# Turning one batch row's tokens in a single iteration, and re-ordering loads, weight splits and constants in a fused linear-attention and mixture-of-experts kernel

## The chip, the cores and the metric

The kernel runs on one core of a Trainium2 chip. The metric is the device time of one execution in microseconds (us). The kernel before took 807.06 us (median of 3 runs, 805.79 to 808.11).

A core has TensorE (PE in the profile, with its weight loads as PEld), VectorE (DVE), ScalarE (ACT), GpSimd (POOL) and SyncE (SP), which here only issues DMAs. Each engine works through its own instructions in their order and waits at one until what it needs is there; the engines are tied by semaphores only.

## The reference

Three layers follow each other, all in float32:

```
# 1. gated linear attention; B, H, S, D = 4, 8, 768, 48
for t in range(S):
    state = alpha[:, :, t, :, None] * state + einsum('bhd,bhe->bhde', k[:, :, t], v[:, :, t])
    y[:, :, t] = einsum('bhd,bhde->bhe', q[:, :, t], state)
x = y.transpose(0, 2, 1, 3).reshape(3072, 384)
# 2. top-1 mixture of 8 experts, 384 -> 1024 -> 384
e = argmax(x @ w_gate, axis=1);  gate = softmax(x @ w_gate)[e]
x = gate * (relu(x @ w1[e]) @ w2[e])
# 3. dense layer, 384 -> 2048 -> 384
h = x @ w_in;  out = (h * sigmoid(h)) @ w_out
```

## The kernel before, in words

**Attention.** The 32 heads are taken in 16 pairs `p` (4 pairs make one batch row `b`), the 768 steps of a head in 6 chunks of 128. For a pair, DVE runs a scan of alpha forward (`Pf`, step P_SCAN) and one backward (`Rv`, R_SCAN); q is multiplied by the first (`qs`, Q_SCALE, on POOL, for pair 0 on DVE) and k by the second (`ks`, K_SCALE, DVE). TensorE then makes the scores inside a chunk (`Ap`; DVE masks them to `Am`), the state updates (`U`; DVE scans them to `So`, ACT copies them to `Sb`), and the output `Yp` from both. The loop `for p in range(NP + 1)` (NP = 16) is a pipeline written out by hand: iteration p prepares pair p+2, loads pair p+3, makes scores and updates of pair p and the outputs of pair p-1. Nothing reorders it: each engine's order is the order in which the code is written. So "iteration 14" below is the piece of code with p = 14, and iteration 16 only finishes pair 15.

**Routing beside it.** Once the four pairs of a batch row are done, the row's 768 tokens are routed beside the next iterations. `beside_pairs(b)` makes a table from (iteration, place) to steps; `aside(p, place)` runs them. The places in an iteration stand in the order A, F1, F2, F3 (between TensorE's groups), C1 and C2 (around R_SCAN). The steps are: `logits`, `choose` (the largest logit, DVE), `weigh` (`w_exp` on ACT, then `w_gate`, which gives `gt`, on DVE), `ranks`, `slots`, `digits`, `hots`, `invert` and `add` (they build the table `tab` of the tokens of each expert), and six times `rows(b, c)`: TensorE turns a chunk of 128 tokens (`Xt`), ACT scales it by the gate into `xr` (four buffers), SP stores it to `x_d` in DRAM. Batch rows 0 and 1 have five iterations for this; batch row 2 (the `else` branch) has three, 13 to 15. At its end `gather_a` (POOL) fetches up to 192 tokens of the first expert from the stored rows of batch rows 0 to 2 into `xg`; it needs `tab` and all of those stores. Batch row 3 is routed after the loop.

**First expert and after.** In iteration 16 `x_rows` turns the gathered tokens (`xt`, `both`), `logits` makes the logits of batch row 3, and `F1(0, 0, CA)` starts the first expert (line 1095). Its weight tiles come from `w_load(t)` (SP, 384 KB into one of 4 `raw` buffers) and `w_split(t)`, which makes a high part `wh` (ACT) and a low part `wl` (DVE; tile 0 on POOL). Tiles 0 to 3 are loaded in iteration 6; `w_load(t+4)` follows `w_split(t)`, since it takes its buffer. While the first expert runs on 192 tokens, batch row 3 is routed, stored and gathered; then 8 experts and the dense layer follow, all on TensorE.

**Start.** `load(p)` issues alpha, k and q of a pair on SP, `load_v(p)` its v; three pairs are loaded before the loop, pair after pair. POOL sets tiles to zero and, in `constants()` (called in iteration 0), makes the small tables of the routing.

Of the kernel before, what the change touches and what calls it, by code (L numbers as in the profile page):

```python
# [9 lines left out]
F32 = mybir.dt.float32  # L10
# [11 lines left out]
B, H, S, D = 4, 8, 768, 48  # L22
NP = B * H // 2
PA = 112
CH = 128
NC = S // CH
SP = NC * (CH + 1)
# [202 lines left out]
def gla_moe_kernel(  # L230
# [12 lines left out]
    nc = tc.nc  # L243
# [84 lines left out]
    def w_split(t, eng=nc.vector):  # L328
        hi, lo = wslot[slot1(t)]
        nc.scalar.copy(hi, raw[t])  # L330
        eng.tensor_tensor(lo, raw.pop(t), hi.bitcast(F32), op=ALU.subtract)  # L331
# [51 lines left out]
    with actx:  # L383
        ac = actx.enter_context(tc.tile_pool(name="ac", bufs=1, reuse_waits="tile"))
        io = actx.enter_context(tc.tile_pool(name="io", bufs=4, reuse_waits="tile"))
        wk = actx.enter_context(tc.tile_pool(name="wk", bufs=2, reuse_waits="tile"))
        am = actx.enter_context(tc.tile_pool(name="am", bufs=5, reuse_waits="tile"))
        st = {}

        def load(p):  # L390
            if p >= NP:
                return
            a_ = io.tile([PA, SP + 1], F32, tag="a", name="a_", bufs=3)
            nc.sync.dma_start(a_, alpha[p])
            k_ = io.tile([PA, S], F32, tag="k", name="k_", bufs=3)
            nc.sync.dma_start(k_, k[p])
            q_ = io.tile([PA, S], F32, tag="q", name="q_", bufs=3)
            nc.sync.dma_start(q_, q[p])
            st[p] = dict(a=a_, k=k_, q=q_)

        def load_first():

            t = [io.tile([PA, n], F32, tag=x, name=x + "_", bufs=3) for x, n in (("a", SP + 1), ("q", S), ("k", S))]
            for c0, c1 in ((0, SP // 2), (SP // 2, SP + 1)):
                nc.sync.dma_start(t[0][:, c0:c1], alpha[0][:, c0:c1])
            nc.sync.dma_start(t[1], q[0])
            nc.sync.dma_start(t[2], k[0])
            st[0] = dict(a=t[0], q=t[1], k=t[2])

        def load_v(p):  # L410
            if p >= NP:
                return
            st[p]["v"] = v_ = io.tile([128, 2 * NC * D], F32, tag="v", name="v_")
            nc.sync.dma_start(v_, v[p])

        for p in range(3):
            load(p) if p else load_first()
            load_v(p)
        Z1 = ac.tile([PA, SP], F32, name="Z1")
        nc.vector.memset(Z1, TINY)  # L420
        nc.vector.memset(Z1[:, 0 : SP : CH + 1], 1.0)
# [5 lines left out]
        nc.gpsimd.affine_select(  # L427
            out=mask, in_=mask, pattern=[[1, 128]], compare_op=ALU.is_ge, fill=0.0, base=0, channel_multiplier=-1
        )
        for t in [D1[0], W[0], Sb[0], D1[1], W[1]]:  # L430
            nc.gpsimd.memset(t, 0.0)
        wgs = xp.tile([PA, 4, 32], F32, name="wgs", bufs=1)
        nc.sync.dma_start(wgs, wg)
# [2 lines left out]
        iota_i, prow_i = ints[:, 0, :].bitcast(I32), ints[:, 1, 0:NTILE].bitcast(I32)  # L436

        def constants():
            for t in [Sb[1], W[2], W[3]]:
                nc.gpsimd.memset(t, 0.0)  # L440
            nc.gpsimd.memset(bm[:, 0:1], -AHI)
            nc.gpsimd.memset(bm[:, 1:2], ALO)
            nc.gpsimd.iota(iota_i, pattern=[[1, 128]], base=0, channel_multiplier=0)
            nc.gpsimd.iota(prow_i, pattern=[[128, NTILE]], base=0, channel_multiplier=1)
            nc.gpsimd.memset(ones, 1.0)
            nc.gpsimd.memset(onesf, 1.0)
            nc.gpsimd.memset(tri, -1.0)
            nc.gpsimd.affine_select(
                out=tri, in_=tri, pattern=[[-1, 128]], compare_op=ALU.is_ge, fill=0.0, base=0, channel_multiplier=1
            )  # L450
            nc.gpsimd.memset(rmask, 1.0)
            nc.gpsimd.memset(ones8, 1.0)
            nc.gpsimd.memset(rmask[:, :, 0:1], 0.0)
            nc.gpsimd.memset(carry, 0.0)
            nc.gpsimd.tensor_copy(iota_f, iota_i)
            nc.gpsimd.tensor_copy(tokid, prow_i)
            nc.gpsimd.tensor_scalar(w8, iota_f[:, 0:E], -1.0, float(E), op0=ALU.mult, op1=ALU.add)
            nc.gpsimd.tensor_scalar(e512, iota_f[:, 0:E], float(TM), None, op0=ALU.mult)
            nc.gpsimd.tensor_scalar(base, iota_f[:, 0:E], float(NF), None, op0=ALU.mult)
            nc.gpsimd.tensor_copy(keys, w8)  # L460
            nc.gpsimd.memset(keys[:, 0:1], 2.0**17)
            for e in range(E):
                nc.gpsimd.memset(caps[:, e : e + 1], float(CAPS[e]))
# [392 lines left out]
        def f(p, i):  # L856
            if p < NP:
                if p not in prs:
                    prs[p] = prep(p)
                prs[p][i]()  # L860
# [5 lines left out]
        def beside_pairs(b):  # L866
            s_, tb = route(b)
            digits, hots, invert, add = tb
            row = [lambda c=c: rows(b, c) for c in range(NC)]
            p = 4 * b + 5  # L870
            at = {
                (p, "A"): [lambda: logits(b), s_["l_copy"]],
                (p, "F2"): [s_["l_turn"]],
                (p, "F3"): [s_["l_rows"]],
                (p, "C1"): s_["choose"],
            }
            if b < B - 2:
                at |= {
                    (p + 1, "F2"): [s_["ranks"]],
                    (p + 1, "F3"): [s_["w_exp"]],  # L880
                    (p + 1, "C1"): [s_["w_gate"]] + s_["slots"],
                    (p + 1, "C2"): [digits],
                    (p + 2, "F2"): [row[0]],
                    (p + 2, "F3"): [row[1]],
                    (p + 2, "C2"): [hots],
                    (p + 3, "F1"): [row[2]],
                    (p + 3, "F2"): [row[3]],
                    (p + 3, "F3"): [row[4], invert],
                    (p + 3, "C1"): [add],
                    (p + 4, "F1"): [row[5]],  # L890
                }
            else:
                at |= {
                    (p, "C2"): s_["weigh"],
                    (p + 1, "A"): [row[0]],
                    (p + 1, "F1"): [row[1]],
                    (p + 1, "F2"): [row[2]],
                    (p + 1, "F3"): [s_["ranks"]],
                    (p + 1, "C1"): s_["slots"],
                    (p + 1, "C2"): [digits, hots],  # L900
                    (p + 2, "A"): [row[3]],
                    (p + 2, "F1"): [row[4]],
                    (p + 2, "F2"): [row[5], invert, add],
                    (p + 2, "F3"): [gather_a],
                }
            return at

# [9 lines left out]
        for p in range(NP + 1):  # L917
            on, oy = p < NP, p >= 1
            load(p + 3)
            if on:  # L920
                for c in range(0, 3):
                    scores(p, c)
            if p == 0:
                constants()
                f(1, R_SCAN)
            f(p + 1, K_SCALE)

            aside(p, "A")
            if p == NP - 1:
                w_split(0, nc.gpsimd)  # L930
                w_load(4)
            if on:
                ks_transpose(p, 0, 3)
            f(p + 2, P_SCAN)
            aside(p, "F1")
            if oy:
                from_states(p - 1, 0)
            aside(p, "F2")
            if on:
                ks_transpose(p, 3, 5)  # L940
            if oy:
                from_states(p - 1, 1)
            aside(p, "F3")
            if p == 0:
                warm(8)
            f(p + 2, Q_SCALE)
            f(p + 2, DECAY)

            if on:
                for c in range(3, 6):  # L950
                    scores(p, c)
                updates(p, 0, 5)
            if oy:
                within(p - 1, 0)
                within(p - 1, 1)
            if on:
                states(p)
            else:
                y_copy(p - 1, 0)
            if oy:  # L960
                y_copy(p - 1, 1)
            if p == 0:
                warm(6)
            aside(p, "C1")
            f(p + 2, R_SCAN)
            aside(p, "C2")
            for t in {NP - 1: (1, 2), NP: (3,)}.get(p, ()):
                w_split(t)
                w_load(t + 4)
            if not on:  # L970
                x_rows(XG[0], XS[0], 0, 0, 128, bank(2, [128, KD, 128], "xt"))
                x_rows(XG[1], XS[0], 1, 0, CA - 128, bank(0, [128, KD, 128], "xt"))
                logits(B - 1)
                last, last_tb = route(B - 1)
                last["l_copy"]()
            load_v(p + 3)
            if p >= 4 and p % 4 == 0 and p < NP:
                for at, todo in beside_pairs(p // 4 - 1).items():
                    plan_r[at] = plan_r.get(at, []) + todo
            if p == 6:  # L980
                for t in range(4):
                    w_load(t)
# [4 lines left out]
    with mctx:  # L987
# [151 lines left out]
        digits, hots, invert, add = last_tb  # L1139
# [290 lines left out]
```

## Time and profile before

| | |
|---|---|
| median of 3 runs | 807.06 us |
| the profiled execution, time | 807.9 us |
| its span, first to last instruction | 806.2 us |
| busy: PE, DVE, ACT, POOL | 771.3, 491.9, 359.4, 143.6 us |
| mean granted TensorE clock | 0.98 |
| HBM read, written | 69.80, 9.44 MB |

A row of the timeline gives start, length, engine, line, operation, output<-input, shape and count; what stands in brackets is how long the engine had been idle before it and what ended that. Start times count from the start of the span. The granted clock of a stretch is 1.00 at 2.4 GHz and 0.50 at 1.2 GHz.

### The profile page before, as it was taken

Reading aid. Unit: us, or ns where it says so; the run is one execution under the profiler, and the core shown is the slowest. Engines: PE = TensorE matmul, PEld = TensorE weight load, DVE = VectorE, ACT = ScalarE, POOL = GpSimd, SP = SyncE. Lnnn points to the kernel's source line nnn. Section 1 sums busy time; section 2 is a strip of 40 time slices with the busy share of each in tenths; the row PEclk is TensorE's granted clock in tenths of the full one; section 3 lists DMA queues with packets and bytes.
Section 4 is the critical chain, followed back from the end, with each engine's and each line's share of the span. In section 5 each row is a group of like instructions: output and inputs, shape, how many; then the busy total and the mean of one; then the engine's idle time right before and its main releaser. Section 6 shows DMA issues by size and latency. Waiting matters only on the chain. (4 is left out here: it accounts for less than half of the span.)

```text
span 806.2 us, 13071 instructions
## 1 busy us (share of the span) xinstructions
PE 771.3 (96%) x5037; PEld 701.1 (87%) x5037; DVE 491.9 (61%) x836; ACT 359.4 (45%) x683; POOL 143.6 (18%) x178
## 2 busy tenths in 40 slices
PE   7898898689999999999999999999999999999995
PEld 5778777589899999999999999989889998899995
DVE  8999997456878877787778533433343333343332
ACT  1455555334444455555544333544444454333322
POOL 4323331131322312311221120020020002002002
PEclk7899999899999999999999999999999999999998
DMA  9768752343546555655321020031012101001001
GB/s 225 185 196 266 228 164 80 113 159 93 168 142 185 162 171 177 188 174 161 114 79 28 28 74 18 1 91 35 1 48 62 35 1 40 2 1 39 1 1 43
DMA packets 40486, 80.17 MB, mean 99 GB/s; under 512 B 4200, under 2 KB 18423, under 8 KB 40416
## 3 DMA queue, kind: packets, MB, share of 16 engines
q1 hardware_dynamic: 36992, 69.33, 29.2%
q0 software_dynamic: 3424, 9.93, 3.7%
q8 instruction: 41, 0.67, 0.4%
q14 instruction: 29, 0.24, 0.1%
HBM read 69.80 MB, written 9.44 MB: 98 GB/s over the span
## 5 line engine op out<-in xcount | busy, mean ns | idle before, releaser
L1095 PE MATMUL hp<-xh,wh 128*128 128x512 f32 (+9 forms) x504 | 184.8, 369 | 0.0
L1095 PE MATMUL hp<-xh,wl 128*128 128x512 f32 (+9 forms) x504 | 183.7, 368 | 0.9 <-DVE wl L331 0.9
L1269 DVE TENSOR_TENSOR sg<-hp,sg 128x512 f32<-128x512 f32 (+1 forms) x97 | 66.5, 686 | 159.5 <-ACT sg L1268 159.4
L1095 PE MATMUL hp<-xl,wh 128*128 128x512 f32 (+9 forms) x504 | 131.1, 368 | 0.0
L1268 ACT ACTIVATE sg<-hp 128x512 f32<-128x512 f32 (+1 forms) x97 | 57.6, 594 | 156.5 <-PE hp L1095 155.7
L1095 PEld LDWEIGHTS hp<-xh,wh 128*128 128x128 f32 x504 | 94.8, 188 | 10.7 <-issue 0.8
L1095 PEld LDWEIGHTS hp<-xl,wh 128*128 128x128 f32 x504 | 91.7, 188 | 13.9
L1095 PEld LDWEIGHTS hp<-xh,wl 128*128 128x128 f32 x504 | 94.8, 188 | 10.2 <-DVE wl L331 1.1
L1278 DVE TENSOR_TENSOR hl<-sg,hh 128x512 fp32r<-128x512 f32 x95 | 65.8, 692 | 61.9 <-PE ob L1290 41.2
L1277 ACT CAST hh<-sg 128x512 fp32r<-128x512 f32 x95 | 58.9, 620 | 71.1 <-DVE sg L1269 71.1
L1104 ACT ACTIVATE hh<-hp 128x192 fp32r<-128x192 f32 (+8 forms) x72 | 34.5, 479 | 115.2 <-PE hp L1095 115.2
L1309 POOL DMA_INDIRECT out_dram<-o,sidx x24 | 24.2, 1009 | 323.2 <-ACT o L1306 318.9
L1022 POOL TENSOR_TENSOR wl<-dx,wh 128x384 fp32r<-128x384 f32 x32 | 38.4, 1199 | 195.6 <-ACT wh L1019 195.6
L331 DVE TENSOR_TENSOR wl<-raw,wh 128x768 fp32r<-128x768 f32 x63 | 61.1, 972 | 9.1 <-ACT wh L330 8.2
L1106 DVE SCALAR_TENSOR_TENSOR hl<-hp,hh 128x192 fp32r<-128x192 f32 (+8 forms) x72 | 38.9, 540 | 43.5 <-ACT hh L1104 43.2
L1290 PE MATMUL both<-wh,hh 128*128 128x384 f32 x190 | 64.4, 339 | 0.0
L1290 PE MATMUL both<-wh,hl 128*128 128x384 f32 x190 | 64.2, 338 | 0.0
L1290 PE MATMUL both<-wl,hh 128*128 128x384 f32 x190 | 63.9, 337 | 0.0
L1290 PE MATMUL ob<-wl,hh 128*128 128x384 f32 x190 | 63.5, 334 | 0.0
L1290 PE MATMUL ob<-wh,hh 128*128 128x384 f32 x190 | 63.5, 334 | 0.0
L1290 PE MATMUL ob<-wh,hl 128*128 128x384 f32 x190 | 63.5, 334 | 0.0
L330 ACT CAST wh<-raw 128x768 fp32r<-128x768 f32 x64 | 52.9, 828 | 0.1
(394 smaller groups left out, 1483.5 us busy)
## 6 DMA issues: line engine op xcount, KB each, us to landing
raw<-in_wt_dram SPq DMA_DIRECT2D x64, 384.0 KB, 3.4
raw<-in_w_dram SPq DMA_DIRECT2D x32, 384.0 KB, 3.1
raw<-in_alpha_dram SPq DMA_DIRECT2D x16, 336.0 KB, 3.4
x_d<-xr SPq DMA_DIRECT2D x24, 192.0 KB, 3.5
xg<-x_d,gidx POOLq DMA_INDIRECT x29, 3.4
out_dram<-o,sidx POOLq DMA_INDIRECT x24, 2.7
a__140<-in_alpha_dram SPq DMA_DIRECT2D x1, 339.1 KB, 7.4
a__148<-in_alpha_dram SPq DMA_DIRECT2D x1, 339.1 KB, 10.4
```

The lines of the kernel that those rows point to most:

```text
L330: nc.scalar.copy(hi, raw[t])
L331: eng.tensor_tensor(lo, raw.pop(t), hi.bitcast(F32), op=ALU.subtract)
L1022: nc.gpsimd.tensor_tensor(r["lo"], r["x"], r["hi"].bitcast(F32), op=ALU.subtract)
L1095: nc.tensor.matmul(hp, lhsT=a[:, kc * 128 : (kc + 1) * 128], rhs=x[:, kc, c0:c1], start=(i == 0), stop=(i == 8))
L1104: nc.scalar.activation(hh[:, :n], hp, AF.Relu)
L1106: nc.vector.scalar_tensor_tensor(hl[:, :n], in0=hp, scalar=0.0, in1=hh[:, :n].bitcast(F32), op0=ALU.max, op1=ALU.subtract)
L1268: nc.scalar.activation(sg[:, z], hp[:, z], AF.Sigmoid)
L1269: nc.vector.tensor_tensor(sg[:, z], hp[:, z], sg[:, z], op=ALU.mult)
L1277: nc.scalar.copy(hh[:, z], sg[:, z])
L1278: nc.vector.tensor_tensor(hl[:, z], sg[:, z], hh[:, z].bitcast(F32), op=ALU.subtract)
L1290: nc.tensor.matmul(yb[tt], lhsT=a[:, tt * 128 : (tt + 1) * 128], rhs=b_[:, 384:768], start=(f == 0 and i == 0), stop=(f == NF2 - 1 and i = ...
L1309: sc = nc.gpsimd.indirect_dma_start(out=out, out_offset=bass.IndirectOffsetOnAxis(ap=sidx[:, i : i + 1], axis=0), in_=ob, in_offset=None,)
```

## The change

- The routing of batch row 2: `weigh` moves from C2 to C1 of iteration 13 (ahead of R_SCAN there), and all six `rows` are in iteration 14 (two at A, one each at F1, F2, F3, the last at C2) instead of three in 14 and three in 15.
- Weights: `w_split(0)` moves from POOL to DVE and behind F1 of iteration 15; `w_load(4)` from A to C2 of iteration 15; `w_split(3)` and `w_load(5)` to `w_load(7)` behind the turning of the gathered tokens and the copy of the logits in iteration 16.
- Loads: alpha, q, k instead of alpha, k, q for every pair, and the first three pairs interleaved.
- Constants: the zeroing of `W[2]` goes to the start, that of `Sb[1]` and `W[3]` stays in iteration 0, `constants()` goes to iteration 2 behind Q_SCALE and DECAY.

```diff
-        def load(p):
-...
-        def load_first():
-...
-        for p in range(3):
-            load(p) if p else load_first()
-            load_v(p)
+        SRC = dict(a=(alpha, [PA, SP + 1], 3), q=(q, [PA, S], 3), k=(k, [PA, S], 3), v=(v, [128, 2 * NC * D], 4))
+
+        def load(p, what="aqk"):
+            for x in what if p < NP else "":
+                src, shape, n = SRC[x]
+                t = st.setdefault(p, {})[x] = io.tile(shape, F32, tag=x, name=x + "_", bufs=n)
+                if x == "a" and p == 0:
+                    nc.sync.dma_start(t[:, 0 : SP // 2], src[p][:, 0 : SP // 2])
+                    nc.sync.dma_start(t[:, SP // 2 :], src[p][:, SP // 2 :])
+                else:
+                    nc.sync.dma_start(t, src[p])
+
         def load_v(p):
+            load(p, "v")
+
+        for p, what in ((0, "aqk"), (1, "aq"), (0, "v"), (1, "k"), (2, "aq"), (1, "v"), (2, "kv")):
+            load(p, what)
...
-        for t in [D1[0], W[0], Sb[0], D1[1], W[1]]:
+        for t in [D1[0], W[0], Sb[0], D1[1], W[1], W[2]]:
             nc.gpsimd.memset(t, 0.0)
...
         def constants():
-            for t in [Sb[1], W[2], W[3]]:
-                nc.gpsimd.memset(t, 0.0)
...
-                    (p, "C2"): s_["weigh"],
-                    (p + 1, "A"): [row[0]],
-                    (p + 1, "F1"): [row[1]],
-                    (p + 1, "F2"): [row[2]],
-                    (p + 1, "F3"): [s_["ranks"]],
+                    (p, "C1"): s_["choose"] + s_["weigh"],
+                    (p + 1, "A"): [row[0], row[1]],
+                    (p + 1, "F1"): [row[2]],
+                    (p + 1, "F2"): [row[3]],
+                    (p + 1, "F3"): [row[4], s_["ranks"]],
                     (p + 1, "C1"): s_["slots"],
-                    (p + 1, "C2"): [digits, hots],
-                    (p + 2, "A"): [row[3]],
-                    (p + 2, "F1"): [row[4]],
-                    (p + 2, "F2"): [row[5], invert, add],
+                    (p + 1, "C2"): [digits, hots, row[5]],
+                    (p + 2, "F1"): [lambda: w_split(0)],
+                    (p + 2, "F2"): [invert, add],
                     (p + 2, "F3"): [gather_a],
+                    (p + 2, "C2"): [lambda: w_split(1), lambda: w_split(2), lambda: w_load(4)],
...
             if p == 0:
-                constants()
+                for t in [Sb[1], W[3]]:
+                    nc.gpsimd.memset(t, 0.0)
                 f(1, R_SCAN)
...
-            if p == NP - 1:
-                w_split(0, nc.gpsimd)
-                w_load(4)
...
             f(p + 2, DECAY)
+            if p == 2:
+                constants()
...
-            for t in {NP - 1: (1, 2), NP: (3,)}.get(p, ()):
-                w_split(t)
-                w_load(t + 4)
             if not on:
...
                 last["l_copy"]()
+                w_split(3)
+                for t in range(5, 8):
+                    w_load(t)
```

(The table's first `p` is 13 here.)

**POOL at the start.** Before, from the last tiles that are zeroed up to the constants (`D_1`, `W_162` to `W_164` and `Sb_166` are `D1[1]`, `W[1]` to `W[3]` and `Sb[1]`; the `qs` are those of pairs 1, 2, ...):

```order
L431 MEMSET D_1_160 112x775
L431 MEMSET W_162 112x288
L498 TENSOR_TENSOR qs<-q__144,Pf 112x768
L440 MEMSET Sb_166 112x672
L440 MEMSET W_163 112x288
L440 MEMSET W_164 112x288
L441 MEMSET bm 112x1
```

The same place now:

```order
L420 MEMSET D_1_160 112x775
L420 MEMSET W_162 112x288
L420 MEMSET W_163 112x288
L485 TENSOR_TENSOR qs<-q__140,Pf 112x768
L912 MEMSET Sb_166 112x672
L912 MEMSET W_164 112x288
L485 TENSOR_TENSOR qs<-q__148,Pf 112x768
L485 TENSOR_TENSOR qs<-q__229,Pf 112x768
L485 TENSOR_TENSOR qs<-q__307,Pf 112x768
L428 MEMSET bm 112x1
```

The constants, which stood between the `qs` of pair 1 and that of pair 2, now stand behind that of pair 4.

**SP around iterations 13 to 16.** Before (`x_d<-xr` are the stores of turned tokens, `raw` the weight loads; in the x5 one store is of batch row 1, the next four and the x2 are of batch row 2, the x6 of batch row 3):

```order
L396 DMA k__1436<-in_k_dram 112x768
L398 DMA q__1438<-in_q_dram 112x768
L844 DMA x_d<-xr 128x384 x3
L414 DMA v__1545<-in_v_dram 128x576
L844 DMA x_d<-xr 128x384 x5
L319 DMA raw<-in_wt_dram 128x768
L844 DMA x_d<-xr 128x384 x2
L319 DMA raw<-in_wt_dram 128x768 x3
L844 DMA x_d<-xr 128x384 x6
```

Now:

```order
L401 DMA q__1436<-in_q_dram 112x768
L401 DMA k__1438<-in_k_dram 112x768
L831 DMA x_d<-xr 128x384 x3
L401 DMA v__1545<-in_v_dram 128x576
L831 DMA x_d<-xr 128x384 x7
L319 DMA raw<-in_wt_dram 128x768 x4
L831 DMA x_d<-xr 128x384 x6
```

The load of weight tile 4 stood ahead of the last two stores of batch row 2 and now stands behind them.

**DVE in iteration 15.** Before, from the end of `hots` (`ol`) over the first half of pair 15's scores to the second:

```order
L779 TENSOR_TENSOR ol<-iota_f,lo 128x768
L537 TENSOR_TENSOR Am<-Ap,mask 128x768
L792 TENSOR_TENSOR tab<-tab,pt 128x32
L847 TENSOR_SCALAR gidx_a<-tab 128x2
L848 TENSOR_SCALAR fl<-carry 1x1
L537 TENSOR_TENSOR Am<-Ap,mask 128x768
```

Now:

```order
L766 TENSOR_TENSOR ol<-iota_f,lo 128x768
L524 TENSOR_TENSOR Am<-Ap,mask 128x768
L331 TENSOR_TENSOR wl_97<-raw,wh_96 128x768
L779 TENSOR_TENSOR tab<-tab,pt 128x32
L834 TENSOR_SCALAR gidx_a<-tab 128x2
L835 TENSOR_SCALAR fl<-carry 1x1
L524 TENSOR_TENSOR Am<-Ap,mask 128x768
```

The low part of weight tile 0 (`wl_97`), which POOL made, is now a DVE instruction ahead of `tab` and of the gather's indices `gidx_a`.

## Rows read from the trace of the kernel before

**Rows 1.** Windows by stage: length, busy us of each engine, granted clock, DMA.
```profile
40.00:120.00 80.00, 73.17 (x992) 62.52 (x990) 78.29 (x111) 43.54 (x92) 22.97 (x19) 0.98 0.73 217
...
138.00:152.72 14.72, 9.00 (x87) 5.61 (x82) 5.47 (x9) 4.83 (x9) 2.60 (x2) 0.77 0.41 136
152.72:180.00 27.28, 24.35 (x216) 23.54 (x214) 15.66 (x50) 10.94 (x26) 7.41 (x7) 1.00 0.45 147
180.00:785.00 605.00, 605.00 (x3186) 558.93 (x3186) 338.92 (x589) 273.17 (x504) 85.80 (x95) 1.00 0.25 77
```
**Rows 2.** Timeline of DVE at the start, pairs 0 to 2.
```profile
8.99 0.96 DVE L510 TENSOR_TENSOR ks<-k__133,Rv 112x768 f32<-112x768 f32 x1
10.56 1.77 DVE L485 TENSOR_TENSOR_SCAN Pf<-a__140,Z 112x774 f32<-112x774 f32 x1 [0.61 <-DMA a__140<-in_alpha_dram]
...
13.38 1.76 DVE L504 TENSOR_TENSOR_SCAN Rv<-a__140,D 112x774 f32<-112x774 f32 x1
15.18 2.20 DVE L510 TENSOR_TENSOR ks<-k__142,Rv 112x768 f32<-112x768 f32 x1
...
23.21 2.00 DVE L510 TENSOR_TENSOR ks<-k__150,Rv 112x768 f32<-112x768 f32 x1
```
**Rows 3.** Timeline of POOL at the start: q scaled of pairs 1, 2, a constant.
```profile
13.51 3.06 POOL L498 TENSOR_TENSOR qs<-q__144,Pf 112x768 f32<-112x768 f32 x1 [9.08 <-DVE Am L537]
...
20.81 1.63 POOL L460 COPY keys<-w 128x8 f32<-128x8 f32 x1
...
22.78 1.62 POOL L498 TENSOR_TENSOR qs<-q__152,Pf 112x768 f32<-112x768 f32 x1
```
**Rows 4.** Timeline of SP: alpha of pairs 1 and 3, weight tile 4.
```profile
3.12 0.43 SPq L394 DMA_DIRECT2D a__140<-in_alpha_dram  x1
...
11.95 0.31 SPq L394 DMA_DIRECT2D a__226<-in_alpha_dram  x1
...
135.60 0.33 SPq L319 DMA_DIRECT2D raw<-in_wt_dram  x1
```
**Rows 5.** DMA issues: size, median us to landing; alpha loads.
```profile
a__140<-in_alpha_dram SPq DMA_DIRECT2D x1, 339.1 KB, 7.4
...
a__226<-in_alpha_dram SPq DMA_DIRECT2D x1, 339.1 KB, 9.6
```
**Rows 6.** DMA issues of 136 to 137 us: the last two stores of batch row 2.
```profile
x_d<-xr SPq DMA_DIRECT2D x2, 192.0 KB, 4.1
```
**Rows 7.** Timeline of ACT in iterations 13 and 15.
```profile
123.76 0.24 ACT L702 ACTIVATE ex<-df 128x48 f32<-128x48 f32 x1
...
132.38 0.58 ACT L842 ACTIVATE xr<-Xt,gt 128x384 f32<-128x384 f32 x1
```
**Rows 8.** Timeline of DVE in iterations 13, 15 and 16.
```profile
123.33 1.74 DVE L504 TENSOR_TENSOR_SCAN Rv<-a__1434,D 112x774 f32<-112x774 f32 x1
...
135.44 0.19 DVE L792 TENSOR_TENSOR tab<-tab,pt 128x32 f32<-128x32 f32 x1 [1.16 <-PE pt L784]
...
137.24 0.96 DVE L537 TENSOR_TENSOR Am<-Ap,mask 128x768 f32<-128x768 f32 x1 [1.36 <-PE Ap L532]
...
143.11 0.96 DVE L331 TENSOR_TENSOR wl<-raw,wh 128x768 fp32r<-128x768 f32 x1
```
**Rows 9.** Timeline of POOL: the first gather.
```profile
141.98 1.69 POOL L344 DMA_INDIRECT xg<-x_d,gidx_a  x1 [6.41 <-DVE wl L331]
```
**Rows 10.** Timeline of PE in iterations 13, 14 and 16.
```profile
114.87 2.14 PE L637 MATMUL Lp<-xb,wgs 112*32 112x256 f32 x24
...
126.40 0.60 PE L839 MATMUL Xt<-ident,xb 112*128 112x112 f32 x4 [1.70 <-ACT xr L842]
...
146.82 0.90 PE L354 MATMUL xt<-ident,xg 128*128 128x128 f32 x3 [4.36 <-DMA xg<-x_d,gidx_a]
148.66 0.58 PE L354 MATMUL both<-ident,xg 64*128 64x64 f32 x3 [0.93 <-DMA xg<-x_d,gidx_a]
149.16 3.63 PE L637 MATMUL Lp<-xb,wgs 112*32 112x256 f32 x24
```

More of the change, by code (lines that the diff above doesn't have):

```diff
@@ L388, in gla_moe_kernel @@
         st = {}
-        def load(p):
[L391 to L399, printed above, removed]
-        def load_first():
[L403 to L408, printed above, removed]
-        def load_v(p):
[L411 to L414, printed above, removed]
-        for p in range(3):
-            load(p) if p else load_first()
-            load_v(p)
+        SRC = dict(a=(alpha, [PA, SP + 1], 3), q=(q, [PA, S], 3), k=(k, [PA, S], 3), v=(v, [128, 2 * NC * D], 4))
[8 more added lines that the diff above has]
+                    nc.sync.dma_start(t, src[p])
+        def load_v(p):
+            load(p, "v")
+        for p, what in ((0, "aqk"), (1, "aq"), (0, "v"), (1, "k"), (2, "aq"), (1, "v"), (2, "kv")):
+            load(p, what)
         Z1 = ac.tile([PA, SP], F32, name="Z1")
```

## The prediction

> **What bounds the kernel now.** I read the windows by stage first, then the timelines of the two stages that the change touches, then the DMA issues.
>
> The windows give three stages [rows 1]. From 40 to 120 us DVE is busy for 78.29 of 80.00 us: the attention pipeline goes at DVE's pace, so what DVE gains or loses near its start is still gained or lost at its end. From 180 to 785 us TensorE is busy for all of 605.00 us at a granted clock of 1.00: whatever reaches it earlier moves the end by as much, and nothing in that stage is edited. Between them, from 138 to 152.72 us, TensorE is busy for 9.00 of 14.72 us at a mean clock of 0.77: neither engine is full, a wait ends last there.
>
> That wait is the gather. TensorE stands 4.36 us before it turns the first gathered tile at 146.82, then 0.93 us before the second [rows 10]. So it had finished the attention at 146.82 - 4.36 = 142.46. The gather began on POOL at 141.98 [rows 9] and the first tile was there 146.82 - 141.98 = 4.84 us later. Its bracket names a DVE weight split, but POOL's gather needs no weight; it needs `tab` (135.44 [rows 8]) and the stores of batch row 2. The last two stores were queued on SP behind the load of weight tile 4, issued at 135.60 [rows 4], and took 4.1 us to land [rows 6], so they landed after 140. The stores were last. The pause also costs clock: the logits that follow take 3.63 us, and the same 24 matmuls took 2.14 us at 114.87 [rows 10].
>
> **The start: loads and constants.** Before, DVE is free at 8.99 + 0.96 = 9.95 and waits for alpha of pair 1, which lands at 3.12 + 7.4 = 10.5 [rows 2, 4, 5]. From there to alpha of pair 3 (11.95 + 9.6 = 21.55) nine transfers land in 11.0 us, 1.2 us each. Alpha of pair 1 now stands one transfer earlier, so it lands at about 9.3, and `Pf` follows at 9.9 instead of 10.56: 0.7 us.
>
> The next two terms come from POOL. Its `qs` of pair 1 ran from 13.51 for 3.06 us against 1.62 for pair 2 [rows 3], while `Rv` held DVE until 15.14; then `ks` of pair 1 took 2.20 us against 0.96 for pair 0 [rows 2], with its end 0.81 us behind the end of that `qs` (16.57). For pair 2, `ks` began at 23.21 and took 2.00 us, ending 0.81 us behind the end of `qs` (24.40). So whichever of the two begins second stands until the first is done. Now q of pair 1 comes before its k, so that `qs` can begin with the end of `Pf`, at about 11.8, and end at 13.4; without the constants in between `qs` of pair 2 begins behind its own `Pf` and is over long before `ks`. Both `ks` then take 0.96 us: 1.24 and 1.04 us less.
>
> Against that, the earlier `qs` of pair 1 now meets `Rv` of pair 1, which would begin at 12.7. No row shows a scan that comes second. Ends: it is not held (0) or held to 13.4 (0.7). I take 0.7, since a POOL operation that met a scan waited (`keys`, 8 columns, 1.63 us [rows 3]) and `ks` did. Sum at the start: 0.7 + 1.24 + 1.04 - 0.7 = 2.3 us.
>
> The Trainium skill ("SBUF — State Buffer", section "Who interferes with whom") has this as a rule: a DVE instruction with two SBUF inputs contends with a GpSimd instruction that reads SBUF, not with one that only writes it, and whoever starts first makes the other stand for the whole instruction. The stretched `qs` and `ks` agree; that a scan is held too is what the rule says and no row does. By the rule the 0.7 is owed, without it the start would give 0.7 more.
>
> The zeroing of `W[2]`, `Sb[1]` and `W[3]` reads nothing and stays in POOL's idle time. The constants now run in iteration 2, in the gap behind `qs` of pair 4 that nothing needs soon; their few operations that read could hold a `ks` or delay the next `qs` (ends 0 and 0.9, of the size of one `ks`; I take 0.1, as each is 0.2 to 0.3 us of work by its width against the 768 columns of `qs`). Later loads keep their distance of three pairs: alpha of pair 3 lands at 21.55, and DVE would want it at 25.1 - 2.3 = 22.8. Swapping k and q there I cost at nothing. Net at the start: 2.2 us, ends 0.7 (both unknowns against it, and the alpha gain lost to a later transfer) and 3.0.
>
> **Iterations 13 to 15.** `weigh` ahead of `Rv` makes DVE wait for the exponential on ACT, done at 123.76 + 0.24 = 124.0, where `Rv` had begun at 123.33 [rows 7, 8]: 0.7 us. Its three small operations only change places. In exchange the gate is ready about 1 us earlier, and TensorE's 1.70 us wait at the third turned tile, for an `xr` that waited for the gate [rows 10], shrinks by about as much. Iteration 14 gets three more turns (0.60 us of TensorE, 0.58 of ACT each [rows 7, 10]); they lie in that wait and in the waits at its end, and I let it end 0.4 us later. Iteration 15 loses them. DVE waited there 1.16 us for the inversion and 1.36 us for scores [rows 8], both behind those turns; the 0.96 us of `wl` for tile 0 (as the one at 143.11 [rows 8]) goes into this. I take 0.9 us back, so TensorE ends the attention 0.5 us earlier, at 142.0 in the old times (ends: 0.7 later, none of the waits shortened, and 1.9 earlier, the two waits minus `wl` and the exponential's wait plus 1 us of the 1.70).
>
> **The gather.** The sixth store's `xr` comes at the end of iteration 14, about where the fourth was (132.38 [rows 7]), by my count at 133.3. With no weight load ahead it lands by 137.4 even at the old 4.1 us. `tab` comes about when it did (hots 0.4 later, the inversion no longer behind turns, `wl` in between): 135.5. The indices follow it, then POOL's own start: about 136.6 (ends 136 and 138.3). That is 5.4 us earlier. At the old 4.84 us the first tile is there at 141.4, before TensorE is (142.0). Weight tile 4 is now issued beside the gather, 384 KB; before, three such loads were. The second tile came 148.66 - 146.82 = 1.84 us behind the first: 143.3 at the latest, while TensorE has turned the first by 142.5. I take a wait of 0.4 (ends 0 and 0.8).
>
> So: 142.0, first turn 0.5 (0.90 at half clock), wait 0.4, second turn 0.35, logits 2.14 at full clock (a wait under 2 us left the clock alone at 126.40; after 4.36 us it was at half) gives 145.4 for the end of the logits, which was 149.16 + 3.63 = 152.8: 7.4 us.
>
> Then `w_split(3)` lies between the logits' copy and `choose` of batch row 3. ACT's part runs beside the first matmuls of the expert; DVE's 0.96 us delays the first `hl` and the routing behind it, 0.5 us after what it overlaps. I charge all 0.5: the routing of batch row 3 feeds the second gather. What is queued behind tile 3 on SP are the stores of batch row 3, over 3 us away. Net: 6.9 us, ends 3.6 (clock at half, 0.45 + 1.49 + 0.25 us for the turns and the logits, and the gather at 138.3, so that its first tile comes 1.1 us after TensorE wants it) and 8.4 (no wait at the second tile, the 0.5 not owed, TensorE there 0.6 earlier, when the gathered tile is).
>
> **Sum.** 2.2 + 6.9 = 9.1 us. The profiled execution took 807.9 us (span 806.2 and 1.7 around it): 798.8. It lay 0.8 above the median, 807.06, so the median to compare with becomes 798.0.
>
> **The rivals.**
> - *The start's gain is lost on the way.* Something else sets the pace of iterations 2 to 12, such as a load or scores at half clock, and only the end pays: 807.06 - 6.9 = 800.2. Against it: DVE's 78.29 of 80.00 us. For it: 1.7 us of idle DVE in that stretch, and alpha of pair 3 with only 1.2 us in hand.
> - *The gather does not get out of the way.* ACT, with five `xr` and four buffers in iteration 14, stands until a store has landed, or POOL starts late; the gather begins only about 2.5 us earlier. TensorE still waits near 2 us and the clock falls: 807.06 - 2.2 - 2.5 = 802.4. For it: 4.1 us for a store. Against it: the stores now have no load ahead of them.
> - *Everything pays more.* `Rv` is not held, no wait at the second tile, the waits of iteration 15 gone, both upper ends: 807.06 - 3.0 - 8.4 = 795.7. For it: no row shows a scan that is held. Against it: it needs four terms to go well at once.
> - *Slower, by the clock.* The split of tile 3 makes the routing of batch row 3 late, TensorE stands in the first expert for about 4 us as it stood for the gather, and the stretch that now runs 152.72 to 180 at clock 1.00 runs in good part at half. It holds 24.35 us of TensorE work [rows 1]; half of it at half clock is 12.2 us more: 807.06 - 9.1 + 12.2 = 810.2. It decides from 9.1 us of such work on. Against it: the delay is 0.5 us, and waits of that size left the clock at 1.00 from 152.72 to 180.
>
> **Chances.** Forecast 0.58 (its own range 796.3 to 800), start lost 0.16, gather still late 0.11, more 0.11, slower 0.04. 0.3% is 2.4 us, about what a measurement can tell from no change: faster needs less than 804.6. The first four cases lie there; I leave 0.04 for smaller gains: faster 0.92, same 0.04, slower 0.04. The range 794.8 to 802.6 takes in the first four.
>
> **What would show it.** At the start: `ks` of pairs 1 and 2 at 0.96 us, and `ks` of pair 2 ending near 23 instead of 25.2. A `Rv` of pair 1 stretched to 2.4 us shows that it was held, one of 1.76 that it was not. In iteration 13 a DVE wait of about 0.7 us for `ex`. Six stores of batch row 2 issued before 134 minus 2.2, the gather near 136.6 - 2.2 = 134.4, no long wait at `xt`, logits in 2.14 us, and their end near 145.4 - 2.2 = 143.2. It would be wrong if TensorE still stands over 2 us for the gather, if the clock is at 0.5 around the logits, or if DVE has lost the start's gain by 120 us.

## The result and the profile after

The changed kernel took 797.18 us (median of 4 runs, 796.64 to 797.26), the kernel before 807.38 us beside it (4 runs): ratio 0.9875, 95% interval 0.9858 to 0.9892, some 10.1 us. Later, on another chip, it took 796.12 us (6 runs) against 808.68: 0.9844 [0.9821, 0.9867]. The forecast was 798.0 us, a gain of 9.1 us. The profiled execution took 796.64 us, its span 794.9, 11.3 less than before.

The windows by stage answer to [rows 1] (the first one, 20 to 40 us, is added):

```profile
20.00:40.00 20.00, 17.62 (x248) 15.00 (x249) 19.90 (x22) 9.53 (x20) 10.13 (x30) 1.00 0.81 219
40.00:120.00 80.00, 70.91 (x979) 60.03 (x978) 77.86 (x115) 43.51 (x93) 23.05 (x19) 1.00 0.67 204
138.00:152.72 14.72, 13.63 (x142) 11.90 (x140) 10.39 (x32) 8.05 (x20) 0.00 (x0) 1.00 0.49 161
152.72:180.00 27.28, 25.55 (x220) 25.08 (x220) 15.55 (x47) 8.42 (x20) 11.21 (x11) 1.00 0.39 125
180.00:785.00 605.00, 604.43 (x3144) 557.12 (x3143) 337.24 (x575) 274.20 (x504) 83.28 (x93) 1.00 0.24 76
```

The pause has gone from 138 to 152.72 us: TensorE is busy for 13.63 of 14.72 us there, at clock 1.00 instead of 0.77. DVE is still the engine that fills 40 to 120 us.

DVE's timeline at the start and in iterations 13 to 16 (answers to [rows 2, 8]):

```profile
8.69 0.96 DVE L497 TENSOR_TENSOR ks<-k__136,Rv 112x768 f32<-112x768 f32 x1
9.56 1.76 DVE L472 TENSOR_TENSOR_SCAN Pf<-a__138,Z 112x774 f32<-112x774 f32 x1
...
12.37 2.30 DVE L491 TENSOR_TENSOR_SCAN Rv<-a__138,D 112x774 f32<-112x774 f32 x1
14.71 0.96 DVE L497 TENSOR_TENSOR ks<-k__144,Rv 112x768 f32<-112x768 f32 x1
...
21.50 0.95 DVE L497 TENSOR_TENSOR ks<-k__152,Rv 112x768 f32<-112x768 f32 x1
...
29.15 1.76 DVE L472 TENSOR_TENSOR_SCAN Pf<-a__305,Z 112x774 f32<-112x774 f32 x1
...
35.95 1.76 DVE L472 TENSOR_TENSOR_SCAN Pf<-a__387,Z 112x774 f32<-112x774 f32 x1
...
39.34 2.56 DVE L491 TENSOR_TENSOR_SCAN Rv<-a__387,D 112x774 f32<-112x774 f32 x1
...
114.46 1.77 DVE L472 TENSOR_TENSOR_SCAN Pf<-a__1434,Z 112x774 f32<-112x774 f32 x1
...
120.59 0.20 DVE L719 TENSOR_REDUCE sm<-ex 128x6 f32<-128x48 f32 x1 [0.62 <-ACT ex L689]
...
143.21 0.96 DVE L331 TENSOR_TENSOR wl<-raw,wh 128x768 fp32r<-128x768 f32 x1 [2.00 <-ACT wh L330]
144.35 0.19 DVE L652 TENSOR_REDUCE mx<-lg 128x6 f32<-128x48 f32 x1
```

Both `ks` are at 0.96 and 0.95 us, as forecast. `Rv` of pair 1 takes 2.30 us instead of 1.76: it was held, as taken. `Rv` of pair 5 (39.34) takes 2.56 us, and nothing in the forecast says so. `mx`, the first step of batch row 3's routing, begins at 144.35; before, it began at 154.71.

POOL's timeline (answers to [rows 3, 9]): `qs` of pair 1, two of the constants in their new place, `qs` of pair 5, the first gather.

```profile
11.41 1.64 POOL L485 TENSOR_TENSOR qs<-q__140,Pf 112x768 f32<-112x768 f32 x1 [6.71 <-DVE Pf L472]
...
35.15 0.93 POOL L444 TENSOR_SCALAR w<-iota_f 128x8 f32<-128x8 f32 x1
36.16 1.59 POOL L445 TENSOR_SCALAR e<-iota_f 128x8 f32<-128x8 f32 x1
...
38.65 1.62 POOL L485 TENSOR_TENSOR qs<-q__389,Pf 112x768 f32<-112x768 f32 x1
...
132.59 1.23 POOL L344 DMA_INDIRECT xg<-x_d,gidx_a  x1 [14.59 <-DVE fl L835]
```

The gather starts right behind the index (`fl`, DVE), 9.4 us earlier than before; no store is waited for.

TensorE's timeline in iteration 16 (answers to [rows 10]):

```profile
136.55 1.35 PE L576 MATMUL Yp<-qs,Sb 112*112 112x128 f32 x10 [1.58 <-ACT Sb L565]
...
139.28 0.55 PE L354 MATMUL xt<-ident,xg 128*128 128x128 f32 x3
139.76 0.40 PE L354 MATMUL both<-ident,xg 64*128 64x64 f32 x3
140.09 1.93 PE L624 MATMUL Lp<-xb,wgs 112*32 112x256 f32 x24
```

No bracket stands behind `xt` or `both`: TensorE waits for neither gathered tile. The logits take 1.93 us, not 3.63. The 1.58 us for `Sb` were 0.44 before:

```profile
139.66 1.35 PE L589 MATMUL Yp<-qs,Sb 112*112 112x128 f32 x10 [0.44 <-ACT Sb L578]
```

The longer wait comes from ACT, which began the copy ahead of `Sb` late:

```profile
135.51 0.48 ACT L608 COPY xb<-Yp 112x384 f32<-112x384 f32 x1 [3.73 <-PE Yp L591]
135.89 0.61 ACT L565 COPY Sb<-So 48x240 f32<-48x240 f32 x1
```

SP's timeline and the DMA issues of 115 to 132 us (answers to [rows 4] and [rows 6]): all seven stores of that stretch, and behind them the weight loads from tile 4 on.

```profile
115.16 14.98 SPq L831 DMA_DIRECT2D x_d<-xr  x7
132.01 12.51 SPq L319 DMA_DIRECT2D raw<-in_wt_dram  x4
```

```profile
x_d<-xr SPq DMA_DIRECT2D x7, 192.0 KB, 1.8
```

Each of these stores lands in 1.8 us, where the two behind the weight load took 4.1 (their median). The load had held those two on SP as well: it waited there for its buffer until POOL's split of tile 0 had ended, at 135.58, while ACT had made the last two `xr` by 134.99. From the trace before:

```profile
133.77 1.81 POOL L331 TENSOR_TENSOR wl<-raw,wh 128x768 fp32r<-128x768 f32 x1 [12.31 <-ACT wh L330]
```

The span's 11.3 us by stage, from start times of the two profiles: DVE begins `Pf` of pair 15 at 114.46 instead of 117.91 (3.45); from there to `mx` it takes 29.89 instead of 36.80 us (6.91); from `mx` to the end 650.55 instead of 651.49 (0.94). The two rows of the trace before:

```profile
117.91 1.76 DVE L485 TENSOR_TENSOR_SCAN Pf<-a__1434,Z 112x774 f32<-112x774 f32 x1
...
154.71 0.19 DVE L665 TENSOR_REDUCE mx<-lg 128x6 f32<-128x48 f32 x1
```

The 0.94 was not forecast, and little of it can be put down to the change: in the later profiles whose clock did not fall behind `mx`, this last stage takes between 650.63 and 651.44 us.

### The profile page after: what moved, and what is told of

Its sections match the earlier page's. It is cut to its first block, busy times and chain, and to the rows that moved or that the text cites. A ratio compares the mean times of both kernels' runs of the same rounds, so it can differ in the third digit from the quotient of the medians.

```text
span 794.9 us, 13069 instructions
## 1 busy us (share of the span) xinstructions
PE 763.8 (96%) x5037; PEld 695.0 (87%) x5037; DVE 491.4 (62%) x837; ACT 359.4 (45%) x683; POOL 141.0 (18%) x177
```

## The experiments

The theory: two independent gains, the start (who comes second on POOL and DVE) and the gather (the stores of batch row 2 behind the load of weight tile 4). Rivals: one of them does it all; the gather is early for another reason than the load; part of the change costs. e1 to e4 ran on one chip (before 807.44 us, 13 runs), e5 to e8 on a second (808.2, 23 runs), e10 and e11 on a third (808.68, 11 runs).

**e1: the second half alone.** The kernel before with the new table, splits and weight loads; loads and constants of the start as before.

```diff
-                    (p, "C2"): s_["weigh"],
...
+                    (p, "C1"): s_["choose"] + s_["weigh"],
+                    (p + 1, "A"): [row[0], row[1]],
...
```

> The kernel before with the second half of the change alone (the table for batch row 2, the weight splits and the weight loads); first loads and constants as before. Theory: the two halves are independent, each pays its own part. In the trace of the changed kernel DVE is 3.4 us ahead at the last forward scan (114.46 against 117.91) and the logits of batch row 3 end 10.8 us earlier, so this half is worth 6.5 to 7.5 us: 800 to 801 us, gather on POOL near 136, logits in about 2 us, and no change of the timeline before 120 us. Rival: the halves need each other (the end only fits because the start left the transfers and the clock in another phase): 803 us or more here, and a TensorE wait for the gather of over 2 us.

Measured: 801.23 us, ratio 0.9909 [0.9879, 0.9940], 0.2 us above the expected range. In its profile `Pf` of pair 15 begins at 118.02, as before, and `mx` at 147.83, 6.9 us earlier than before (forecast 6.9):

```profile
140.03 1.35 PE L589 MATMUL Yp<-qs,Sb 112*112 112x128 f32 x10 [1.53 <-ACT Sb L578]
142.76 0.55 PE L354 MATMUL xt<-ident,xg 128*128 128x128 f32 x3
...
143.57 1.93 PE L637 MATMUL Lp<-xb,wgs 112*32 112x256 f32 x24
```

**e2: the start alone.** New load order and constants; the rest as before.

```diff
-        for p in range(3):
-            load(p) if p else load_first()
-            load_v(p)
+        for p, what in ((0, "aqk"), (1, "aq"), (0, "v"), (1, "k"), (2, "aq"), (1, "v"), (2, "kv")):
+            load(p, what)
...
+            if p == 2:
+                constants()
```

> The kernel before with the first half of the change alone (order of the loads, constants in iteration 2); routing and weights as before. Theory: DVE sets the pace from 9 to 120 us, so the 3.4 us that it is ahead by then in the changed kernel arrive at the end in full: 803.5 to 804.5 us, with the same 4.4 us TensorE wait for the gather and logits in 3.6 us at half clock. Rival: the start's gain is taken back, since the gather's wait at the end would absorb what arrives earlier: 806.5 to 807.5 us, the wait at the gather grown to 7 us.

Measured: 805.53 us, 0.9980 [0.9967, 0.9993], between the two. `Pf` of pair 15 begins at 115.18, 2.7 us earlier than in the profile before, and TensorE then waits longer for the gather that is still late:

```profile
145.56 0.90 PE L354 MATMUL xt<-ident,xg 128*128 128x128 f32 x3 [5.80 <-DMA xg<-x_d,gidx_a]
```

5.80 instead of 4.36 us [rows 10]: 1.4 us of what the start gained are spent there, and 0.9 of them come back at the second tile, which TensorE no longer waits for; up to `mx` 0.6 us are lost (37.42 us from `Pf` of pair 15, 36.80 before). The gather itself began 2.9 us earlier on POOL (139.04), but its first tile was there 6.5 us after that instead of 4.8; why is open. The two halves' ratios multiply to 0.989; the whole measured 0.9875.

**e3: one line.** The kernel before with the load of weight tile 4 behind the last two stores of batch row 2, and nothing else.

```diff
             if p == NP - 1:
                 w_split(0, nc.gpsimd)
-                w_load(4)
...
+            if p == NP - 1:
+                w_load(4)
             for t in {NP - 1: (1, 2), NP: (3,)}.get(p, ()):
```

> The kernel before with one line moved: the load of weight tile 4 is issued behind the last two stores of batch row 2 (end of iteration 15) instead of ahead of them. Turned rows, splits, loads and constants as before. Theory: the gather waited for these two stores only because they stood behind that load on SP until 135.6; their data was ready at about 134.5 and 135.0. They then land by about 137.5, the gather starts near 138.4 instead of 142.0, TensorE waits under 1.5 us for it and the logits keep full clock: a gain of 4.5 to 6.5 us, 801 to 803 us. Rival: the rows themselves are turned too late (three of them in iteration 15) and the load only happened to stand there: a gain under 2 us, 805.5 us or more.

Measured: 799.81 us, 0.9915 [0.9883, 0.9946], better than I expected: as much as the whole second half. POOL's gather and TensorE's first tile:

```profile
136.40 1.23 POOL L344 DMA_INDIRECT xg<-x_d,gidx_a  x1 [2.29 <-DMA x_d<-xr]
...
141.49 0.55 PE L354 MATMUL xt<-ident,xg 128*128 128x128 f32 x3
```

The gather still waits for the last store, but that lands 1.9 us after its issue; TensorE does not wait. So the load ahead of two stores was the whole cause of the pause. Not all of the gain in this profile is the edit's: its clock did not fall around 30 us as it had before (more on this below), and `Pf` of pair 15 began at 116.43 instead of 117.91; from there to `mx` the edit gave 7.15 us (29.65 instead of 36.80).

**e4: the table alone.** The kernel before with `weigh` at C1 and all six `rows` in iteration 14; splits and weight loads where they were.

```diff
+                    (p, "C1"): s_["choose"] + s_["weigh"],
+                    (p + 1, "A"): [row[0], row[1]],
+                    (p + 1, "F1"): [row[2]],
...
```

> The kernel before with only the table for batch row 2 changed (weigh in C1, six rows in iteration 14); the split of tile 0 stays on POOL and all weight loads stay where they were. Theory: with all six stores issued in iteration 14 the load of tile 4 has nothing left to hold up, so this alone gives the gather's start near 136 to 137 and a gain of 6 to 7.5 us, 800 to 801.5 us; moving the weight loads and the split to DVE adds nothing to it (within 1 us of the whole second half). Rival: the moved splits and loads carry a good part: 803 us or more here.

Measured: 798.18 us, 0.9892 [0.9865, 0.9918], better than the expected 800 to 801.5 us; here too the clock stayed up around 30 us, and `Pf` of pair 15 began at 115.70. The stores come out ahead of the load by being earlier:

```profile
133.98 1.23 POOL L344 DMA_INDIRECT xg<-x_d,gidx_a  x1 [0.33 <-DVE fl L848]
...
139.87 0.55 PE L354 MATMUL xt<-ident,xg 128*128 128x128 f32 x3
```

Either edit alone (e3 or e4) removes the wait; together they do not pay twice (e1: 0.9909, and the three intervals overlap).

**e5 and e6: the start in two.** e5 has the new order of loads alone, e6 the constants alone (diffs: the two parts of e2's).

> The kernel before with the new order of the first loads alone; constants, table, splits and later loads as before. If the start's gain is who-comes-second on POOL and DVE: `qs`(1) goes first, `Rv`(1) is held to about 2.3 us, `ks`(1) takes 0.96 instead of 2.20; the constants still stand ahead of `qs`(2), so `ks`(2) stays near 2.0. Lead at the start 0.6 (alpha of pair 1) + 1.24 - 0.5 = 1.3 us, of which the gather's wait takes a part as it did with the whole start change (it paid 1.9 of 2.1 to 2.8): 806.1 to 806.6. Rival: the whole of the start change is the loads: 805.5. Rival: nothing without the constants: 807.4.

> The kernel before with the constants in iteration 2 and `W[2]` zeroed early, all else as before. If a late `qs`(2) is what stretches `ks`(2): `ks`(2) falls from 2.00 to 0.96, and `Rv`(5) is held 0.8 us by the `qs`(5) that the constants now delay: lead 0.2 us, 807.0 to 807.4. Rival: the constants are the whole of the start's gain: 805.5. Rival: they cost: 808.

Measured: e5 804.66 us, 0.9967 [0.9947, 0.9988]; e6 808.18, 0.9999 [0.9980, 1.0018]. The loads carry the start's gain, more of it than I expected; the constants pay nothing. DVE in e5 and in e6:

```profile
13.43 2.29 DVE L493 TENSOR_TENSOR_SCAN Rv<-a__138,D 112x774 f32<-112x774 f32 x1
15.76 0.96 DVE L499 TENSOR_TENSOR ks<-k__144,Rv 112x768 f32<-112x768 f32 x1
...
22.64 1.48 DVE L499 TENSOR_TENSOR ks<-k__152,Rv 112x768 f32<-112x768 f32 x1
```

```profile
15.57 2.20 DVE L508 TENSOR_TENSOR ks<-k__142,Rv 112x768 f32<-112x768 f32 x1
...
23.60 0.95 DVE L508 TENSOR_TENSOR ks<-k__150,Rv 112x768 f32<-112x768 f32 x1
...
41.44 2.56 DVE L502 TENSOR_TENSOR_SCAN Rv<-a__387,D 112x774 f32<-112x774 f32 x1
```

e5 mends `ks` of pair 1 (0.96), e6 that of pair 2 (0.95), and e6 alone has the stretched `Rv` of pair 5: the constants win 1.05 us at pair 2 and lose 0.8 at pair 5. Counted from `Rv` of pair 0 to `Pf` of pair 15, at full clock around 30 us, the old start takes 108.47 and 108.96 us (e3 and e4), e6 108.80, e5 107.29 and both parts together (e2) 107.57: in the traces too, the constants add nothing to the loads.

**e7: start and table.** The changed kernel's start and table; the splits of tiles 0 to 3 and the loads of tiles 4 to 7 as before.

```diff
-                    (p + 2, "F1"): [lambda: w_split(0)],
...
-                    (p + 2, "C2"): [lambda: w_split(1), lambda: w_split(2), lambda: w_load(4)],
```

> The start change (load order and constants) and the new table of rows; the splits of tiles 0 to 3 and the loads of tiles 4 to 7 stay where they were before (split 0 on GpSimd). If the moved splits and loads add nothing: gather without a wait at `xt`, split 3 back in DVE's idle time ahead of the logits, so that the routing of batch row 3 comes 0.4 us earlier, and the `Sb` wait of iteration 16 falls from 1.58 to about 0.9: 796.2 to 796.8, under the changed kernel. Rival: the loads must be out of the way once the start is earlier too: the gather's wait is back by 1 us or more and the time is 798 to 799.5.

Measured: 796.08 us, 0.9858 [0.9834, 0.9882], just under what was expected if the moved splits and loads add nothing. Split 3 is back ahead of the routing:

```profile
138.84 0.96 DVE L331 TENSOR_TENSOR wl<-raw,wh 128x768 fp32r<-128x768 f32 x1
142.71 0.19 DVE L652 TENSOR_REDUCE mx<-lg 128x6 f32<-128x48 f32 x1
```

**e8: the constants in two parts.** The changed kernel; what follows the triangle goes to iteration 3.

```diff
+        def constants_2():
             nc.gpsimd.memset(rmask, 1.0)
...
-            if p == 2:
-                constants()
+            if p in (2, 3):
+                (constants if p == 2 else constants_2)()
```

> The changed kernel with its constants in two parts: up to the triangle in iteration 2, the casts, small scalings and caps in iteration 3. If the constants cost 0.8 us by delaying `qs`(5) to 38.65, which then holds `Rv`(5) to 2.56: `qs`(5) begins with the end of `Pf`(5), near 37.7, `Rv`(5) takes 1.75, and the end comes 0.8 earlier, 796.4. Rival: the 0.8 us is taken back by a later wait, or the second part holds another pair: 797.2.

Measured: 795.83 us, 0.9839 [0.9817, 0.9862]. POOL and DVE at pair 5:

```profile
38.20 1.64 POOL L487 TENSOR_TENSOR qs<-q__389,Pf 112x768 f32<-112x768 f32 x1 [3.44 <-PE U L540]
...
39.71 1.76 DVE L493 TENSOR_TENSOR_SCAN Rv<-a__387,D 112x774 f32<-112x774 f32 x1
```

`qs` now begins 1.5 us ahead of `Rv`, not 0.7, and `Rv` takes 1.76 us: the mechanism is shown. One constant of the second part (`keys`, 1.50 us beside `Pf` of pair 6) now delays `qs` of pair 6 to 45.19, which holds `Rv` of that pair (46.50) to 1.94; 0.6 us are left. The interval is too wide to show them in the time.

**e10 and e11: both, beside the changed kernel.** e10 is e7 with e8's split of the constants; e11 is the changed kernel, unchanged.

> The start change and the new table of rows, splits and loads where they were before, and the constants in two parts (iterations 2 and 3). If the two gains are separate places of the kernel (`Rv`(5) at 1.76, worth 0.8 at the start; split 3 in DVE's idle time, worth 0.4 to 0.5 after the logits), they add: 795.3 or 0.5 to 0.8 under the kernel with either of them alone, and 1.2 to 1.5 under the changed kernel of the same call. Rival: the gather or another wait takes the second one back: the time of the constants in two parts alone, 0.8 or less under the changed kernel.

> The changed kernel again, beside the run above on one chip. If the 1.58 us that TensorE stood for `Sb` in iteration 16 belongs to one execution (ScalarE began a copy 1.1 us after its input), it is near 0.44 here and the profiled time is about 1 us less, 795.6 to 796.2. If the moved load of weight tile 4 causes it, it is there again: 796.6 to 797.3.

Measured: e10 795.84 us, 0.9842 [0.9817, 0.9866]; e11 796.12, 0.9844. No difference can be told; each interval is 2 us wide on either side. In e11 TensorE's wait for `Sb` is 0.44 us, and in e8, with the moved load as well, it is the same, while e1 had 1.53. So the 1.58 belongs to single executions and does not follow from the moved load:

```profile
135.57 1.35 PE L576 MATMUL Yp<-qs,Sb 112*112 112x128 f32 x10 [0.44 <-ACT Sb L565]
```

e10 has `mx` at 142.36, 1.0 us ahead of e11 (143.37), and ends 1.6 us later (its profiled execution took 797.28 us, above its median). TensorE stands 1.29 us for the second gather there, 0.83 in e11, and then runs at half clock, in e10 alone:

```profile
163.42 0.40 PE L354 MATMUL xt<-ident,xg 64*128 64x64 f32 x3 [1.29 <-DMA xg<-x_d,gidx]
```

```profile
164.00:167.00 3.00, 3.00 (x15) 3.00 (x15) 0.36 (x1) 0.17 (x1) 0.91 (x1) 0.50 0.37 112
```

In e7, e8, e10 and e11 the second gather begins on POOL 12.47 to 12.48 us behind `mx`, so it moves along with the logits. TensorE begins to turn the tile of it that it waits for 8.26, 8.65, 8.58 and 7.92 us after that (at 163.44, 163.85, 163.42 and 163.76). So up to 0.7 us of what came earlier goes between the gather's start and its tile, and TensorE's wait there, 0.83 to 1.55 us, is what is left to gain in this place. What sets that landing time is open.

## Why the prediction was right, and where not

**The gather: right in its cause, its size right partly by luck.** Forecast 136.6 in the old times; e1, whose start is the old one, has 136.13. The clock stayed at 1.00 and the logits took 1.93 us (2.14 taken). Two misses cancel. TensorE came to the gathered tile at 139.28 + 3.45 = 142.7 in the old times, 0.7 later than forecast, since it stood 1.1 us more for `Sb`; from there to the logits' end it took 2.74 us instead of 3.4, without the wait taken at the second tile. So this half gave 6.91 us, against 6.9. Without the late copy (e11: from 114.64 to 143.37, 28.73 us against 36.80) it gives 8.1, near the forecast's upper end of 8.4. e3 shows what the forecast named without proof: the load ahead of the stores.

**`weigh` earlier: its cost right, its gain half.** It cost 0.62 us of DVE's wait, 0.7 taken. TensorE's wait at the third turned tile fell from 1.70 to 1.21 us, where about 1 us less was forecast. **Split 3 behind the logits: right.** From the logits' end to `mx` 2.33 us against 1.92: 0.4, 0.5 charged; e7 has it at 1.85.

**The start: three terms right, the constants wrong, one gain not seen.** Up to `Pf` of pair 4 (29.15 against 31.91) the lead is 2.76 us, forecast 2.3: `Pf` of pair 1 comes 1.0 earlier instead of 0.7 (its wait of 0.61 is gone, and pair 0 was done 0.3 earlier), the two `ks` 1.24 and 1.05 as worked out, the held `Rv` costs 0.54, 0.7 taken. The 0.3 is luck: the loads of pair 0 are the same, and its `Rv` begins between 6.74 and 7.96 in the twelve profiles. Counted from there, `Pf` of pair 1 comes 0.69 earlier, as forecast. No row had shown a scan that is held; the trace of the change does (2.30 us), and e5 as well (2.29). The rule in the Trainium skill ("SBUF — State Buffer", section "Who interferes with whom") says so of any DVE instruction with two SBUF inputs that meets a GpSimd instruction which reads SBUF; the trace agrees with it.

The step that failed is the constants "at 0.1 us". Their operations were priced by width. In iteration 2 some of them came second to DVE and stood: the one at 35.15 took 0.93 us for eight columns beside `ks` of pair 4, the one at 36.16 took 1.59 us, as `Pf` of pair 5 ran from 35.95 for 1.76 (in their old place these two took 0.19 and 0.26). So the constants lasted to 38.65, `qs` of pair 5 began 0.7 us ahead of `Rv`, and `Rv` paid 0.8. The price lay inside the forecast's own ends (0 to 0.9); the row of `keys` (1.63 us [rows 3]) was there to take the upper end.

The gain not seen is 1.5 us of clock. In the profile before, TensorE stood 1.52 us for `Am` of the pair behind the late `ks`, and then ran at half clock, which DVE waited for:

```profile
28.10 0.94 PE L532 MATMUL Ap<-qs,ks 48*128 48x128 f32 x12 [1.52 <-DVE Am L537]
```

```profile
30.00:36.00 6.00, 6.00 (x51) 5.52 (x53) 5.05 (x7) 1.72 (x4) 1.63 (x1) 0.50 0.53 126
```

From `Pf` of pair 4 to that of pair 5 it took 8.35 us; after, 6.80, with that wait at 0.48 us and the clock at 1.00. It does not belong to every execution: e4, with the old start and the same wait of 1.52 us, kept its clock at 1.00, and e1 lost it after a wait of only 1.01 us there. So 2.76 + 1.55 - 0.80 = 3.5 us at `Pf` of pair 15 (3.45 measured); against e4's and e3's profiles, whose start is the old one at full clock, it is 1.24 and 1.97 (from 115.70 and 116.43 to 114.46), and counted from `Rv` of pair 0, 1.39 and 0.90 (107.57 after). So of the 2.2 us forecast for the start the edit itself gave about 0.9 to 1.4; the rest of the 3.45 is clock and luck.

**The sum.** The forecast of 9.1 us lies inside the measured interval (8.7 to 11.5 us of 807.38). The two mechanisms are right, but that the size came out so near is in part luck: in the profile the constants (0.7 more than charged) and TensorE's late arrival at the gathered tile (0.7) stand against clock (1.55, not in every execution), the shorter way from that tile to the logits' end (0.66), pair 0 (0.3) and the 0.94 behind `mx`.

**The rivals.** "The start's gain is lost on the way" held in part for e2 alone, where 0.6 us of it were gone by `mx`, not for the whole change. "The gather does not get out of the way" is refuted by e1, e3 and e4. "Everything pays more" (795.7, a gain of 11.4 us) was near in size: the runs of e11 show 12.6 us (interval 10.8 to 14.5). By e11's profile that came by way of the clock and of the full second half, while `Rv` was held. "Slower, by the clock" did not come: 1.00 from 138 to 180.

## What to carry to other kernels

When a gather waits for stores, look at what stands ahead of those stores in their DMA queue before moving any work: here one weight load, moved by a few lines, gave as much as a new table of steps, within what the runs can tell (0.9915 and 0.9892). A small operation on POOL can stand for as long as the DVE operation that it comes second to: price it by that, and look at whom it delays in its own queue. A gain can be waited away at the next transfer (in e2 at the first gather, whose tile came 1.3 us earlier where the attention's last scan was 2.7 earlier), so read the arrival there before adding further edits.

## What was not expected of the hardware

Two engines' long operations trade places from run to run. With the old start, POOL's `qs` of pair 1 came second in the profile before (3.06 us) and first in e1, where DVE's `Rv` took 3.22 us instead of 1.76; 0.04 us decided (13.37 and 13.41).

TensorE's clock fell to 0.50 behind short waits in some executions and not in others: behind the wait for the second gather it fell after 1.23, 1.29, 1.37 and 1.40 us (e5, e10, e6, e1) and stayed at 1.00 after 0.80, 1.14, 1.26 and even 1.55 us (after, before, e4, e8). The length of the wait does not decide it alone; what does stays open. Why ACT began its copy 1.1 us late in one profile of the changed kernel and in e1, and not in e8 and e11, is open too.
